# MLP's first product: the tail's low-by-high products as 64-row pairs

## The chip, the cores and the metric

The kernel runs on one core of one Trainium2 chip. The core has five engines with instruction queues of their own: TensorE (PE, matrix products, with its weight loads listed as PEld), VectorE (DVE), ScalarE (ACT), GpSimd (POOL) and SyncE (SP, which issues the DMAs). Engines run their queues in order and wait for each other by semaphores. The metric is the device time of one execution in microseconds (us); the time before is 894.02 us, the median of 3 runs from 894.0 to 894.94.

## The reference

Two pairs of layers: linear attention, then an MLP with gelu, each behind a layernorm and with a residual. S = 2048 tokens, D = 448, F = 1792, 16 heads of 28.

```python
def _B_ref(x, w1, b1, w2, b2):
    h = jnp.einsum("bsd,df->bsf", x, w1) + b1
    h = _gelu(h)
    return jnp.einsum("bsf,fd->bsd", h, w2) + b2
x = A_x
x = x + _A_ref(_layernorm(x, axis=-1), A_wqkv, A_wo)
x = x + _B_ref(_layernorm(x, axis=-1), B_w1, B_b1, B_w2, B_b2)
x = x + _A_ref(_layernorm(x, axis=-1), A_wqkv, A_wo)
x = x + _B_ref(_layernorm(x, axis=-1), B_w1, B_b1, B_w2, B_b2)
```

`_A_ref` is the linear attention. All arrays are float32.

## The kernel before

**Precision.** Every float32 operand of a large product is split into a high part, rounded to the type that TensorE takes at full speed (float32r), and a low part, the rest. A product a·b becomes three: hi·hi, hi·lo, lo·hi.

**Tiling.** D = 448 is contracted as three chunks of 128 rows and a tail of 64. For the tail, the activations hold the 64 rows twice, one copy over the other, and the weights hold hi over lo in 128 rows (`w1x`). So one product of 128 rows gives x_hi·(w_hi + w_lo), and a second one x_lo·(w_hi + w_lo), of which x_lo·w_lo is more than the three terms need.

**Stages of a layer.** Phase 1 goes over 16 token tiles of 128 for k, v and q (`proj`, `stage_g` and others), while w1 and w2 are loaded and split in the background (`bg_pieces`: ScalarE rounds the high part, GpSimd subtracts for the low one). A short transition turns the attention's sums into a matrix. Then the MLP runs over NB = 4 blocks b of 512 tokens, and in each block over NF = 14 chunks i of 128 columns of F:

- `mlp1(l, b, i)`: 11 products of 512 columns into one bank of PSUM, tag `h` with two banks taken in turn (L699 to L701 for the three chunks of D, L702 and L703 for the tail); then gelu on ScalarE into `g` (L705), its high part `gh` by a cast on ScalarE (L708, tag A, two buffers), its low part `gl` on VectorE (L709, tag B, two buffers).
- `mlp2(l, b, i, acc)`: 12 products of 448 columns, three for each of the four token tiles (L717, L718 with `gh`, L719 with `gl`), summed over the 14 chunks in four banks.
- `behind(l, b, i, tr)`: the attention's output and the layernorm of the next block (or the one behind it), a few steps in each i by a table written out by hand: `PLAN_0` for b = 0, `PLAN_1` for b = 1, `PLAN` for b = 2. Its steps: `z` (`q_z`, GpSimd), `p` (`q_prep`: VectorE scales q and turns it in 32x32 squares), `sq` and `lq` (to memory and back), `q` (`q_part`: the cast of qh on ScalarE and the subtraction for ql on VectorE, L269 and L270), `o` (`oc_mm`: 11 products, L651 to L655, then `o_ln` on VectorE, L660 and the statistics), `n` (`m_prep`: normalizes and turns, L190, L251, L252), `sx`, `lx` and `x` (`m_part`: the splits XH on ScalarE and XL on VectorE, L269 and L270, from which mlp1 of the next block reads). Of the plans: block 0 has "o1 n0 q2 ld0" at i = 6, "o2 n1 sx0 q3" at 7, "x1 p0 z1" at 11 and "x2 x3 p1 sq0 z2" at 12; block 1 has "o2 n1 sx0 q3" at 4, "o3 n2 lx0 ld0" at 5, "x2 p2 z3 lq0" at 10 and "x3 p3 sq1" at 11.

The order in each engine's queue is the order of the calls (the schedule is manual). In step i it is mlp1 of chunk i+1 (or of chunk 0 of the next block), `background(1)` in the first block of the first layer, the steps of `behind`, then mlp2 of chunk i.

Of the kernel before, what the change touches and what calls it, by code (L numbers as in the profile page):

```python
# [10 lines left out]
F32R = mybir.dt.float32r  # L11
AF = mybir.ActivationFunctionType
OP = mybir.AluOpType
# [9 lines left out]
def linear_attn_mlp_kernel(  # L23
# [12 lines left out]
    pe, act, dve, pool, sp = nc.tensor, nc.scalar, nc.vector, nc.gpsimd, nc.sync  # L36
    x0 = x_in[0]
    y_out = out[0]
    S, D = x0.shape
    F = w1.shape[1]  # L40
    H, DH = 16, 28
    NT = S // 128
    NB = NT // 4
    NF = F // 128
# [17 lines left out]
    def bank(tag, bufs, name):  # L62
        return psum.tile([128, 512], F32, name=name, tag=tag, bufs=bufs)
# [3 lines left out]
    def t448(tag, bufs, name, dt=F32):  # L67
        bufs = NH if tag == "H" else bufs
        return work.tile([128, D], dt, name=name, tag=tag, bufs=bufs)

    def t512(tag, bufs, name, dt=F32):
        return work.tile([128, 512], dt, name=name, tag=tag, bufs=bufs)

    def f(ap):
        return ap.bitcast(F32)
# [4 lines left out]
    def load_x(l, t):  # L80
        xt[l, t] = t448("H", 8, f"x{l}_{t}")
        sp.dma_start(xt[l, t], x_d[l][t * 128:(t + 1) * 128, :])
# [5 lines left out]
    def stage_piece(src, c, eng, s):  # L88

        if c < 3:  # L90
            eng.dma_start(s, src[c * 128:(c + 1) * 128, :])
        else:
            eng.dma_start(s[0:64], src[TL:D, :])
            eng.dma_start(s[64:128], src[TL:D, :])
        return s
# [69 lines left out]
    b1s = consts.tile([128, NF], F32, name="b1s")  # L165
# [4 lines left out]
    w1x = wts.tile([128, F], F32R, name="w1x")  # L170
# [44 lines left out]
    blocks = {}  # L215
# [80 lines left out]
    def bg_pieces():  # L296
        n = 0

        def stage():
            nonlocal n  # L300
            n += 1
            if n <= LATE:
                return t512("xn", 2, "stg")[:, :D]
            return t448(f"W{5 + n % 2}", 1, "stg")

        for fc in range(4):
            sl = slice(fc * D, (fc + 1) * D)
            for c in range(4):
                s = stage_piece(w1[:, sl], c, sp, stage())

                def go(c=c, s=s, sl=sl):
                    if c < 3:
                        act.copy(w1h[:, c, sl], s)
                        pool.tensor_tensor(w1l[:, c, sl], s, f(w1h[:, c, sl]), op=OP.subtract)
                    else:
                        tmp = t512("e", 3, "bx", F32R)[:, :D]
                        act.copy(tmp, s)
                        act.copy(w1x[0:64, sl], s[0:64])
                        pool.tensor_tensor(w1x[64:128, sl], s[64:128], f(tmp[64:128]), op=OP.subtract)
                yield go  # L320
        for i in range(NF):
            s = stage()
            sp.dma_start(s, w2[i * 128:(i + 1) * 128, :])

            def go(i=i, s=s):
                act.copy(w2h[:, i], s)
                pool.tensor_tensor(w2l[:, i], s, f(w2h[:, i]), op=OP.subtract)
            yield go
# [4 lines left out]
    def background(n):  # L333
        while bg_wait:
            bg_wait.pop(0)()
        for _ in range(n):
            g = next(bg, None)
            if g is not None:
                bg_wait.append(g)
# [78 lines left out]
    def stage_q(l, t):  # L418
        if t is None:
            return  # L420
        qo.append((l, t, proj("q", ("a", l, t // 4), t % 4)))
# [173 lines left out]
    def load_pq(l, b, j):  # L595
        t = b * 4 + j
        pqt[l, t] = t448(f"W{j}", 1, f"pq{l}_{t}")
        sp.dma_start(pqt[l, t], pq_d[l][t * 128:(t + 1) * 128, :])

    def q_z(l, b, j, tr):  # L600
        pz = pzs[l, b, j] = t448(f"W{4 if b else 4 + j % 2}", 1, "pz")
        pool.tensor_tensor(pz, pqt[l, b * 4 + j], tr.zb, op=OP.mult)  # L602
# [87 lines left out]

    gs = {}

    def mlp1(l, b, i):
        hp = bank("h", 2, "hp")
        s = slice(i * 128, (i + 1) * 128)
        x = blocks["m", l, b]
        o = hp.rearrange("p (t n) -> p t n", t=4)
        for c in range(3):
            pe.matmul(o, w1h[:, c, s], x.moving(x.hi, c), start=(c == 0), stop=False)  # L699
            pe.matmul(o, w1l[:, c, s], x.moving(x.hi, c), start=False, stop=False)  # L700
            pe.matmul(o, w1h[:, c, s], x.moving(x.lo, c), start=False, stop=False)  # L701
        pe.matmul(o, w1x[:, s], x.moving(x.hi, 3), start=False, stop=False)  # L702
        pe.matmul(o, w1x[:, s], x.moving(x.lo, 3), start=False, stop=True)  # L703
        g = t512("e", 3, "g")
        act.activation(g, hp, AF.Gelu_apprx_tanh, bias=b1s[:, i:i + 1])  # L705
        gh = t512("A", 2, "gh", F32R)
        gl = t512("B", 2, "gl", F32R)
        act.copy(gh, g)  # L708
        dve.tensor_sub(gl, g, f(gh))  # L709
        gs[i] = (gh, gl)  # L710

    def mlp2(l, b, i, acc):
        gh, gl = gs.pop(i)
        first, last = i == 0, i == NF - 1
        for j in range(4):
            s = slice(j * 128, (j + 1) * 128)
            pe.matmul(acc[j], gh[:, s], w2h[:, i], start=first, stop=False)  # L717
            pe.matmul(acc[j], gh[:, s], w2l[:, i], start=False, stop=False)  # L718
            pe.matmul(acc[j], gl[:, s], w2h[:, i], start=False, stop=last)  # L719
            if last:  # L720
                t = b * 4 + j
                xs = xt.pop((l, t))
                dve.tensor_tensor(xs, acc[j], xs, op=OP.add)
                sp.dma_start(x_d[l + 1][t * 128:(t + 1) * 128, :], xs)
# [95 lines left out]
    for l in range(LAYERS):  # L820
        tr = SimpleNamespace(mp={})
        za, acc = phase1(l, tr)
        if l == 0:
            background(0)
        fill = list(range(DEFER, NT))

        def pre(j):
            for k in range(4):
                load_pq(l, 1, k)
            q_z(l, 1, 0, tr)  # L830

        tok_ = SimpleNamespace(
            Q=lambda j: stage_q(l, fill.pop(0)), Qp=lambda j: stage_qphi(), G=lambda j: stage_g(l, NT - 1, acc),
            ld=lambda j: (load_pq(l, 0, j), load_x(l, j)), z=lambda j: trans_z(tr, za), gt=lambda j: trans_gt(tr, acc),
            kv=lambda j: trans_kv(tr), mask=lambda j: trans_mask(tr), m=lambda j: trans_m(tr, j),
            ms=lambda j: trans_ms(tr, j), qz=lambda j: q_z(l, 0, j, tr), qs=lambda j: q_scale(l, 0, j, tr),
            tq=lambda j: q_transpose(l, 0, j), qq=lambda j: q_split(l, 0, j), o=lambda j: o_mm(l, 0, j, tr),
            la=lambda j: o_ln(l, 0, j), lb=lambda j: o_n(l, 0, j), T=lambda j: m_transpose(l, 0, j),
            x=lambda j: m_split(l, 0, j), pre=pre)
        for tok in ORDER.split():  # L840
            name, j = tok.rstrip("0123456789"), int("0" + tok.lstrip("abcdefghijklmnopqrstuvwxyzQTG"))
            getattr(tok_, name)(j)
        assert not fill and not qo

        mlp1(l, 0, 0)
        trans_chunks(tr)
        for b in range(NB):
            acc = [bank("acc", 4, f"y{j}")[:, :D] for j in range(4)]
            nxt = b + 1 < NB
            if not nxt and l + 1 < LAYERS:  # L850
                st_k = stage_square(wqkv[:, D:2 * D])
                st_q = stage_square(wqkv[:, :D])
                load_to(l + 1, PRE - 1)
            for i in range(NF):
                if i + 1 < NF:
                    mlp1(l, b, i + 1)
                elif nxt:
                    mlp1(l, b + 1, 0)
                if l == 0 and b == 0:
                    background(1)  # L860
                if nxt:
                    behind(l, b, i, tr)
                elif l + 1 < LAYERS:
                    if i == 2:
                        split_kq("k", st_k)
                    if i == 5:
                        split_kq("q", st_q)
                    if i in (3, 4, 6, 7, 8):
                        t = (3, 4, 6, 7, 8).index(i)
                        stage_a(l + 1, t)  # L870
                        stage_n(l + 1, t)
                        stage_t(l + 1, t)
                        if t % 2:
                            stage_sp(l + 1, t)
                    if 9 <= i < 13:
                        stage_x(l + 1, i - 9)
                mlp2(l, b, i, acc)
# [28 lines left out]
```

## Time and profile before

| | |
|---|---|
| median of 3 runs | 894.02 us (894.0 to 894.94) |
| profiled execution | 896.46 us |
| its span on the core | 894.7 us |
| granted TensorE clock | 0.996 of full speed |
| instructions in the profile | 11665 |
| HBM traffic | 100 GB/s over the span |

The profile shows one execution. Its parts are the busy time of each engine, the chain of work that ended last (followed back from the last instruction to what released each step), groups of equal instructions with the idle time of the engine ahead of them and what ended it, and the timeline of single instructions: start in us, duration in us, engine, line, operation, output<-inputs, shape, count, and in brackets the idle time of the engine ahead of it and what released it. Matmuls overlap in the array: the recorded length of one is longer than the distance from its start to the next one's.

### The profile page before, as it was taken

The numbers are of one execution on the slowest core, as the hardware profiler recorded it, in microseconds if no ns is written. First come the engines' busy times: TensorE is split into PE (matmuls) and PEld (weight loads), VectorE is DVE, ScalarE is ACT, GpSimd is POOL, SyncE is SP. The second block draws the span as 40 slices with busy tenths as digits, with TensorE's granted clock in tenths as the row PEclk, the third lists the DMA queues.
The fourth block names the chain that finished last, engine by engine and source line by source line (L and its number), as shares of the span: only waits on it lengthen the run. The fifth ranks groups of instructions, "written<-read, shape, count | busy, mean of one in ns | idle before, by whom it ended". The sixth has DMA issues, their size and how long they took to land.

```text
span 894.7 us, 11665 instructions
## 1 busy us (share of the span) xinstructions
PE 878.8 (98%) x4184; PEld 772.8 (86%) x4184; DVE 502.3 (56%) x970; ACT 339.5 (38%) x586; POOL 209.1 (23%) x243
## 2 busy tenths in 40 slices
PE   7999999999999999999999999999999999999998
PEld 6898988888788888888889998888878888888887
DVE  6897686655754544226469866864565473532112
ACT  4677744333222322333345564343132233223221
POOL 4576723322112012002023333320310210210000
PEclk8999999999999999999999999999999999999999
DMA  6386622623513412051135542053233223010001
GB/s 175 121 244 220 194 82 92 208 76 102 170 52 92 143 33 80 16 175 48 47 127 196 173 123 82 32 178 112 65 106 132 91 92 130 34 62 20 22 1 42
DMA packets 62762, 93.71 MB, mean 105 GB/s; under 512 B 8816, under 2 KB 57968, under 8 KB 62704
## 3 DMA queue, kind: packets, MB, share of 16 engines
q1 hardware_dynamic: 62704, 92.97, 32.9%
q8 instruction: 33, 0.54, 0.3%
q14 instruction: 25, 0.20, 0.1%
HBM read 55.65 MB, written 34.08 MB: 100 GB/s over the span
## 4 chain that ended last, share of the span: by engine, by line
PE 84%; DVE 7%; issue 2%; DMA 2%; ACT 2%; POOL 2%; SPq 1%; POOLq 0%; DVEq 0%; ACTq 0%
PE y L719 10%; PE y L717 10%; PE y L718 10%; PE hp L701 8%; PE hp L700 8%; PE hp L699 8%; PE hp L703 3%; PE hp L702 3%; PE G L436 2%; PE G L437 2%; PE G L435 2%; PE op L652 2%; PE op L651 2%; PE op L653 2%; PE psk L281 2%
## 5 line engine op out<-in xcount | busy, mean ns | idle before, releaser
L709 DVE TENSOR_TENSOR gl<-g,gh 128x512 fp32r<-128x512 f32 x112 | 78.5, 701 | 303.6 <-ACT gh L708 303.5
L705 ACT ACTIVATE g<-hp,b1s 128x512 f32<-128x512 f32 x112 | 77.1, 688 | 400.7 <-PE hp L703 400.6
L717 PE MATMUL y<-w2h,gh 128*128 128x448 f32 x448 | 163.8, 366 | 1.7 <-ACT g L705 1.7
L719 PE MATMUL y<-w2h,gl 128*128 128x448 f32 x448 | 163.8, 366 | 0.5 <-DVE gl L709 0.5
L718 PE MATMUL y<-w2l,gh 128*128 128x448 f32 x448 | 163.6, 365 | 0.0
L701 PE MATMUL hp<-XL,w1h 128*128 128x512 f32 x336 | 131.3, 391 | 0.3 <-DVE XL L270 0.3
L699 PE MATMUL hp<-XH,w1h 128*128 128x512 f32 x336 | 131.5, 391 | 0.1
L700 PE MATMUL hp<-XH,w1l 128*128 128x512 f32 x336 | 131.6, 392 | 0.0
L183 POOL TENSOR_TENSOR brs<-bve,mhalf 128x1 f32<-128x1 f32 x64 | 39.8, 622 | 320.4 <-DVE bve L181 318.3
L717 PEld LDWEIGHTS y<-w2h,gh 128*128 128x128 f32 x448 | 84.1, 188 | 11.4 <-ACT g L705 2.5
L718 PEld LDWEIGHTS y<-w2l,gh 128*128 128x128 f32 x448 | 84.1, 188 | 8.3
L719 PEld LDWEIGHTS y<-w2h,gl 128*128 128x128 f32 x448 | 84.2, 188 | 7.5 <-DVE gl L709 0.9
L701 PEld LDWEIGHTS hp<-XL,w1h 128*128 128x128 f32 x336 | 63.1, 188 | 14.8 <-DVE XL L270 1.2
L699 PEld LDWEIGHTS hp<-XH,w1h 128*128 128x128 f32 x336 | 63.1, 188 | 11.8 <-ACT XH L269 0.8
L700 PEld LDWEIGHTS hp<-XH,w1l 128*128 128x128 f32 x336 | 63.1, 188 | 11.2
L708 ACT CAST gh<-g 128x512 fp32r<-128x512 f32 x112 | 69.7, 622 | 3.6
L602 POOL TENSOR_TENSOR pz<-pq,zb 128x448 f32<-128x448 f32 x32 | 37.1, 1162 | 105.2 <-DVE dn L608 74.0
L666 POOL TENSOR_TENSOR x<-x,b2b 128x448 f32<-128x448 f32 x32 | 36.9, 1152 | 31.5 <-DVE xm L190 23.3
L702 PE MATMUL hp<-XH,w1x 128*128 128x512 f32 x112 | 43.6, 389 | 0.0
L703 PE MATMUL hp<-XL,w1x 128*128 128x512 f32 x112 | 43.6, 389 | 0.0
L177 DVE BATCH_NORM_STATS2 bst<-x 128x6 f32<-128x448 f32 x64 | 39.8, 622 | 6.3 <-DMA x<-in_A_x_dram 5.2
L389 POOL TENSOR_TENSOR xnl<-x,xnh 128x384 fp32r<-128x384 f32 x32 | 35.4, 1107 | 29.6 <-ACT xnh L388 23.0
(144 smaller groups left out, 1581.1 us busy)
## 6 DMA issues: line engine op xcount, KB each, us to landing
x<-in_A_x_dram SPq DMA_DIRECT2D x32, 224.0 KB, 4.0
pq_d<-eq SPq DMA_DIRECT2D x32, 224.0 KB, 2.2
pq<-pq_d SPq DMA_DIRECT2D x32, 224.0 KB, 3.2
x<-x_d SPq DMA_DIRECT2D x32, 224.0 KB, 3.3
sq_a<-sq SPq DMA_DIRECT2D x13, 512.0 KB, 2.6
sp<-sq_a SPq DMA_DIRECT2D x52, 128.0 KB, 3.0
sq_q<-sq SPq DMA_DIRECT2D x12, 512.0 KB, 2.6
sp<-sq_q SPq DMA_DIRECT2D x48, 128.0 KB, 3.0
```

Source lines behind the costliest of these rows:

```text
L177: dve.bn_stats(st, xs)
L699: pe.matmul(o, w1h[:, c, s], x.moving(x.hi, c), start=(c == 0), stop=False)
L700: pe.matmul(o, w1l[:, c, s], x.moving(x.hi, c), start=False, stop=False)
L701: pe.matmul(o, w1h[:, c, s], x.moving(x.lo, c), start=False, stop=False)
L702: pe.matmul(o, w1x[:, s], x.moving(x.hi, 3), start=False, stop=False)
L703: pe.matmul(o, w1x[:, s], x.moving(x.lo, 3), start=False, stop=True)
L705: act.activation(g, hp, AF.Gelu_apprx_tanh, bias=b1s[:, i:i + 1])
L708: act.copy(gh, g)
L709: dve.tensor_sub(gl, g, f(gh))
L717: pe.matmul(acc[j], gh[:, s], w2h[:, i], start=first, stop=False)
L718: pe.matmul(acc[j], gh[:, s], w2l[:, i], start=False, stop=False)
L719: pe.matmul(acc[j], gl[:, s], w2h[:, i], start=False, stop=last)
```

## The change

The two products of the tail stay, but the second (x_lo) takes only the 64 rows of `w1x` that hold the high part. It is put off until two chunks have their other 10 products, and then both chunks' 64-row products are issued one behind the other. So that the two lie in different halves of the array's rows, `w1x` holds hi over lo in chunks of even number and lo over hi in chunks of odd number. The x_lo·w_lo term of those chunks is no longer computed. The two gelus are issued after the pair.

`mlp1_ahead` replaces the call of mlp1 in step i. It brings forward one chunk more: steps 0, 2, 4, 6, 8 and 10 end with the pair (i+1, i+2), ahead of `behind` and of mlp2(i). For blocks 1 and 2 chunk 13 pairs with chunk 0 of the next block at i = 12, and chunk 1 of the next block is begun at i = 13. Chunk 0 of blocks 0 and 1 and chunk 13 of blocks 0 and 3 keep the whole product (`whole`). That is 26 pairs and 4 whole products in each layer.

In the background work the tail of w1 comes in pieces of 512, 512, 512 and 256 columns instead of four of 448, and each is split in two turns (even chunks, odd chunks).

```diff
-                        tmp = t512("e", 3, "bx", F32R)[:, :D]
+                        tmp = t512("e", 3, "bx", F32R)[:, :sl.stop - sl.start]
                         act.copy(tmp, s)
-                        act.copy(w1x[0:64, sl], s[0:64])
-                        pool.tensor_tensor(w1x[64:128, sl], s[64:128], f(tmp[64:128]), op=OP.subtract)
+                        o, a, h = (v.rearrange("p (k u n) -> p k u n", u=2, n=128) for v in (w1x[:, sl], s, tmp))
+                        for u in range(2):
+                            hi, lo = slice(u * 64, u * 64 + 64), slice(64 - u * 64, 128 - u * 64)
+                            act.copy(o[hi, :, u], a[hi, :, u])
+                            pool.tensor_tensor(o[lo, :, u], a[lo, :, u], f(h[lo, :, u]), op=OP.subtract)
...
-    def mlp1(l, b, i):
-        hp = bank("h", 2, "hp")
+    hps = {}
+
+    def mlp1(l, b, i, whole=False):
+
+        hp = hps[b, i] = bank("h", 2, "hp")
...
         pe.matmul(o, w1x[:, s], x.moving(x.hi, 3), start=False, stop=False)
-        pe.matmul(o, w1x[:, s], x.moving(x.lo, 3), start=False, stop=True)
+        if whole:
+            pe.matmul(o, w1x[:, s], x.moving(x.lo, 3), start=False, stop=True)
+            gelu(b, i)
+
+    def mlp1_pair(l, *ends):
+
+        for b, i in ends:
+            x, rows = blocks["m", l, b], slice(i % 2 * 64, i % 2 * 64 + 64)
+            pe.matmul(hps[b, i].rearrange("p (t n) -> p t n", t=4), w1x[rows, i * 128:(i + 1) * 128],
+                      x.moving(x.lo, 3)[rows], start=False, stop=True)
+        for b, i in ends:
+            gelu(b, i)
+
+    def gelu(b, i):
         g = t512("e", 3, "g")
-        act.activation(g, hp, AF.Gelu_apprx_tanh, bias=b1s[:, i:i + 1])
+        act.activation(g, hps.pop((b, i)), AF.Gelu_apprx_tanh, bias=b1s[:, i:i + 1])
         gh = t512("A", 2, "gh", F32R)
         gl = t512("B", 2, "gl", F32R)
         act.copy(gh, g)
         dve.tensor_sub(gl, g, f(gh))
         gs[i] = (gh, gl)
 
+    def mlp1_ahead(l, b, i):
+
+
+        joined = 1 <= b < NB - 1
+        if i == 0:
+            if not 1 < b:
+                mlp1(l, b, 1)
+            mlp1(l, b, 2)
+            mlp1_pair(l, (b, 1), (b, 2))
+        elif i < 11 and i % 2:
+            mlp1(l, b, i + 2)
+        elif i < 11:
+            mlp1(l, b, i + 2)
+            mlp1_pair(l, (b, i + 1), (b, i + 2))
+        elif i == 11:
+            mlp1(l, b, 13, not joined)
+        elif i == 12 and joined:
+            mlp1(l, b + 1, 0)
+            mlp1_pair(l, (b, 13), (b + 1, 0))
+        elif i == 13 and joined:
+            mlp1(l, b + 1, 1)
+        elif i == 13 and b + 1 < NB:
+            mlp1(l, b + 1, 0, True)
...
-        mlp1(l, 0, 0)
+        mlp1(l, 0, 0, True)
...
             for i in range(NF):
-                if i + 1 < NF:
-                    mlp1(l, b, i + 1)
-                elif nxt:
-                    mlp1(l, b + 1, 0)
+                mlp1_ahead(l, b, i)
```

More of the change, by code (lines that the diff above doesn't have):

```diff
@@ L297, in bg_pieces, with stage @@
         n = 0
-        def stage():
+        def stage(wd=D):
             nonlocal n
@@ L302, in stage @@
             if n <= LATE:
-                return t512("xn", 2, "stg")[:, :D]
+                return t512("xn", 2, "stg")[:, :wd]
             return t448(f"W{5 + n % 2}", 1, "stg")
         for fc in range(4):
-            sl = slice(fc * D, (fc + 1) * D)
             for c in range(4):
-                s = stage_piece(w1[:, sl], c, sp, stage())
+                wd = D if c < 3 else 512
+                sl = slice(fc * wd, min((fc + 1) * wd, F))
+                s = stage_piece(w1[:, sl], c, sp, stage(wd)[:, :sl.stop - sl.start])
                 def go(c=c, s=s, sl=sl):
```

## The prediction

> **What bounds the kernel now.** I read the head of the page first, then the chain of waits, the groups of instructions, and the timeline of each engine around the places that the change touches.
>
> ```profile
> span 894.7 us, 11665 instructions
> PE 878.8 (98%) x4184; PEld 772.8 (86%) x4184; DVE 502.3 (56%) x970; ACT 339.5 (38%) x586; POOL 209.1 (23%) x243
> PE 84%; DVE 7%; issue 2%; DMA 2%; ACT 2%; POOL 2%; SPq 1%; POOLq 0%; DVEq 0%; ACTq 0%
> L709 DVE TENSOR_TENSOR gl<-g,gh 128x512 fp32r<-128x512 f32 x112 | 78.5, 701 | 303.6 <-ACT gh L708 303.5
> L708 ACT CAST gh<-g 128x512 fp32r<-128x512 f32 x112 | 69.7, 622 | 3.6
> L703 PE MATMUL hp<-XL,w1x 128*128 128x512 f32 x112 | 43.6, 389 | 0.0
> ```
>
> TensorE sets the end: 98% busy and 84% of the chain. VectorE (56%) looks free, but it holds 7% of the chain, so there are places where TensorE waits for it. What one product costs is the distance between starts, not its recorded length:
>
> ```profile
> 311.27 0.36 PE L717 MATMUL y<-w2h,gh 128*128 128x448 f32 x1
> 313.70 0.39 PE L699 MATMUL hp<-XH,w1h 128*128 128x512 f32 x1
> 316.21 0.36 PE L717 MATMUL y<-w2h,gh 128*128 128x448 f32 x1
> ```
>
> From 311.27 to 313.70 stand the 12 products of mlp2: 0.2025 us each, 2.43 together. From 313.70 to 316.21 stand the 11 of mlp1: 0.228 each. So an L703 product costs 0.228, though its record is 0.389 long.
>
> **The change part by part.** *The half products.* The change takes no instruction from TensorE: 26 pairs a layer, 52 in all, replace two L703 products of 128 rows by two of 64 rows, in the two halves of the array and two banks. The other 8 of the 112 stay whole. If both halves run fully together, a pair costs 0.228 instead of 0.456: 52 × 0.228 = 11.9 us saved. If they run one after the other, nothing is saved. No row of this trace shows a 64-row product, so the value lies between, and the nearest rows are those where the array's weights change fast or late:
>
> ```profile
> 140.49 0.36 PE L283 MATMUL psq<-wq,XL 128*128 128x448 f32 x1
> 140.69 0.60 PE L228 MATMUL tp<-ident,xm 128*128 128x128 f32 x4
> L228 PE MATMUL tp<-ident,xm 128*128 128x128 f32 x32 | 4.9, 276 | 1.0 <-DVE xm L190 0.6 <-DVE XL L235 0.4
> 89.48 0.47 PE L436 MATMUL G<-kl,xnh 128*128 128x448 f32 x1
> 89.79 0.36 PE L437 MATMUL G<-kh,xnl 128*128 128x448 f32 x1
> ```
>
> Four transposes of 128 columns span 0.60 and one lasts 0.276, so they start (0.60 - 0.276) / 3 = 0.108 apart. At 89.48 a product that had waited lasts 0.47 instead of 0.36, and the next starts 0.31 later instead of 0.20. Both say the same: a weight load that nothing hides costs about 0.11. I take it that the second half's weights load only once the first half has started: the pair costs 0.11 + 0.228 and saves 0.118, 52 × 0.118 = 6.1 us. For the other end I take a full drain where the array goes from whole to half and back: each exposes 0.389 - 0.228 = 0.161, so a pair that is otherwise perfect loses 0.322 - 0.228 = 0.094, 4.9 us in all.
>
> The Trainium skill, TensorEngine Tiling (Array Packing), Key Properties, says that a change of tiling mode, as against a change of tile, drains the TensorE. No run here shows such a change yet; by that rule the pairs would lose the 4.9 us. The Trainium skill, TensorE: Matmul & The Clock Gate, Part 3 (The mechanism), has matmuls in different row groups start about 4 ns apart; by that one they would save the 11.9.
>
> *The new wait.* Pairs form two chunks at a time, so both gelus of a pair are issued after it. The tiles gh and gl have two buffers each, which chunks take in turn. At even i the pair (i+1, i+2) stands ahead of mlp2(i), so the cast of gh for chunk i+2 takes the buffer that mlp2(i) still reads; in the changed program's order that cast waits for the L718 product of the fourth output in mlp2(i), the 11th of 12. Before, gh for i+1 took the buffer of i-1, whose readers were done. Behind the waiting cast stand, on ScalarE, all casts of the work for the next block; behind gl on VectorE stand o_ln, the turn of m_prep and the split ql of q_part. TensorE waits for ql and for XL. With T as the start of mlp2(i): the 11th product starts at T + 10 × 0.2025, ends 0.36 later, the cast takes 0.62, and with two handovers of 0.03 gl starts at T + 3.07.
>
> *Place a: o2 in block 0 (i=7), o3 in block 1 (i=5).* Before, in the same step:
>
> ```profile
> 186.62 0.69 DVE L709 TENSOR_TENSOR gl<-g,gh 128x512 fp32r<-128x512 f32 x1 [0.76 <-ACT gh L708]
> 187.47 0.62 DVE L660 TENSOR_TENSOR x<-op,x 128x448 f32<-128x448 f32 x1 [0.16 <-PE op L655]
> ...
> 190.12 0.27 DVE L252 STREAM_TRANSPOSE sq<-xm 128x128 f32<-128x128 f32 x1
> 190.31 1.35 DVE L270 TENSOR_TENSOR ql<-sp,qh 128x512 fp32r<-128x512 f32 x1
> 187.27 0.37 PE L717 MATMUL y<-w2h,gh 128*128 128x448 f32 x1
> 192.63 0.36 PE L653 MATMUL op<-wq,ql 128*128 128x448 f32 x1
> ```
>
> From the start of gl to the end of ql: 191.66 - 186.62 = 5.04, less the 0.16 in which VectorE waited for TensorE, 4.88. TensorE needs ql at 192.63: only 0.97 to spare, although the engine is 56% busy. In the change gl starts at T + 3.07 and ql ends at T + 7.95, while TensorE wants it after mlp2 (2.43), ten products of mlp1 (2.28) and two of oc_mm (0.41), at T + 5.12. It waits 2.83, and 0.11 more for the weights: 2.94. The other ten ql of a layer are issued in an odd step, a step earlier, or with no o_ln ahead of them, and fit. Twice a layer: 5.9.
>
> *Place b: the first chunk of block 1.* Before:
>
> ```profile
> 218.03 0.69 DVE L709 TENSOR_TENSOR gl<-g,gh 128x512 fp32r<-128x512 f32 x1 [3.65 <-ACT gh L708]
> 218.65 0.69 DVE L270 TENSOR_TENSOR XL<-sp,XH 128x512 fp32r<-128x512 f32 x1
> ...
> 222.10 0.27 DVE L252 STREAM_TRANSPOSE sq<-pq 128x128 f32<-128x128 f32 x1
> 222.98 0.69 DVE L709 TENSOR_TENSOR gl<-g,gh 128x512 fp32r<-128x512 f32 x1 [0.60 <-ACT gh L708]
> 223.58 1.29 DVE L270 TENSOR_TENSOR XL<-sp,XH 128x512 fp32r<-128x512 f32 x2
> 223.63 0.37 PE L719 MATMUL y<-w2h,gl 128*128 128x448 f32 x1
> 224.04 0.51 PE L699 MATMUL hp<-XH,w1h 128*128 128x512 f32 x1
> 224.38 0.39 PE L700 MATMUL hp<-XH,w1l 128*128 128x512 f32 x1
> 224.93 0.50 PE L701 MATMUL hp<-XL,w1h 128*128 128x512 f32 x1 [0.15 <-DVE XL L270]
> 225.27 0.40 PE L699 MATMUL hp<-XH,w1h 128*128 128x512 f32 x1
> 231.85 0.39 PE L703 MATMUL hp<-XL,w1x 128*128 128x512 f32 x1
> 233.09 0.44 PE L717 MATMUL y<-w2h,gh 128*128 128x448 f32 x1 [0.86 <-ACT g L705]
> 233.37 0.36 PE L718 MATMUL y<-w2l,gh 128*128 128x448 f32 x1
> ```
>
> Already now this start loses 0.21 + 0.11 + 0.32 + 0.11 (starts from 223.63 to 225.27, less 0.2025 or 0.228 each) = 0.75, and the first gelu of the block another 1.02 + 0.08 = 1.10. The second goes away, because two chunks of mlp1 now stand ahead of mlp2(0). The first grows: gelu(13) is issued at i=11, so gh and gl of chunk 13 wait for mlp2(11), and behind gl stand the split x1, the whole q_prep and the splits x2 and x3. From 218.03 to 222.37 that chain takes 4.34, the last two splits 1.32: x3 is done at T + 3.07 + 5.66 = T + 8.73. TensorE wants it after mlp2(11), mlp2(12) and two products, T + 5.32. It waits 3.41 + 0.11 = 3.5. Net of the two old waits: 3.5 - 0.75 - 1.10 = 1.65.
>
> *Place c: from block 1 to block 2.* There the first chunk of the next block is taken at i=12, one step earlier than before. With T the start of mlp2(10), x3 is done at T + 3.07 + 4.34 + 0.03 + 0.68 = T + 8.12; wanted at 2.43 + 2.28 + 2.43 + 0.46 = T + 7.60. It waits 0.5 + 0.1 = 0.6. Block 3's first chunk has no q_prep ahead of it, and loses nothing.
>
> Together 5.9 + 1.65 + 0.6 = 8.15 a layer, 16.3 in both.
>
> *The split of w1's tail* in phase 1:
>
> ```profile
> L319 POOL TENSOR_TENSOR w1x<-stg,bx 64x448 fp32r<-64x448 f32 x4 | 4.6, 1156 | 0.3
> L390 POOL TENSOR_TENSOR xnh<-x,xnh 128x64 fp32r<-128x64 f32 x32 | 14.9, 466 | 0.0
> ```
>
> Four subtractions become eight, six of 256 columns and two of 128. Between 0.466 at 64 and 1.156 at 448 columns, 256 give 0.81 and 128 give 0.58: 6.0 us instead of 4.6, and four more casts on ScalarE. It lies beside phase 1's products; if TensorE comes to wait for POOL it costs up to the 1.4 plus the casts, at most 2, at least 0. I take 0.6.
>
> Sum: +16.3 + 0.6 - 6.1 = +10.8 us. The profiled execution has a span of 894.7 and took 896.46 in all; the median of the runs is 894.02, so the sum goes on that: 894.0 + 10.8 = 904.8, say 905.
>
> **The rivals.** *Halves fully side by side:* 894.0 + 16.9 - 11.9 = 899. For it: the two halves use different rows and banks, and weight loads run under products everywhere in this trace. Against it: no load here is ever two ahead of its product. *The change doesn't do what it says, the halves follow one another:* 894.0 + 16.9 = 911. For it: the two products stand one behind the other in one queue, as all do here; against it: nothing that they use is shared. *Drains at both borders:* 894.0 + 16.9 + 4.9 = 916. For it: every record here is 0.161 longer than its slot, so something is still in the array when the next product enters. Against it: the transposes at 140.69, another use of the array, start right behind the last product (140.49 + 0.20). (The Trainium skill's rule on tiling modes, named above, is this case.) *Faster:* VectorE and ScalarE take the late gl without TensorE noticing, as their shares (56% and 38%) and the 303.6 us in which VectorE idles ahead of gl suggest. Then places a and c cost nothing, the start of block 1 keeps its 0.75 and loses its 1.10 twice: 894.0 + 0.6 - 6.1 - 2.2 = 886. It decides for faster wherever the added waits stay under what the pairs save, that is if gl's delay of some 3.7 us past its old place (start at T - 0.65, now T + 3.07) finds that much slack in the chains behind it. The 0.97 us at ql speaks against it.
>
> **How the numbers follow.** Partly hidden second half, 905: 0.35, with 902 to 908 as its own range. Fully side by side, 899: 0.25. One after the other, 911: 0.15. Drains, 916: 0.17. No added waits, 886: 0.08. The range from 898 to 917 leaves out the last and some tails. A measurement of this kernel tells 0.2% (1.8 us) from no change; slower has the first four, 0.92 less 0.02 for the side-by-side case with waits that come out 4 us smaller: slower 0.90, same 0.02, faster 0.08.
>
> **What would show it.** Pairs: the distance from the first half's start to the next whole product, 0.34 by the forecast, 0.23 to 0.24 side by side, 0.46 in sequence, 0.55 with drains. Waits: at even i the cast of gh for chunk i+2 idles until mlp2(i) ends; four waits of about 3 us for ql at the third product of oc_mm, two of about 3.5 us for XL at the start of block 1, and the 1.1 us wait for the first gelu of block 1 gone. TensorE's busy share falls, and VectorE and ScalarE do about the same work. I would be wrong if ql is ready in time in block 0, or if pairs cost more than two whole products.

## The result, and the profile after

| | before | after |
|---|---|---|
| median | 894.01 us (893.9 to 894.94, 4 runs) | 925.86 us (924.71 to 931.32, 4 runs) |
| ratio | | 1.0367, 95% interval 1.0346 to 1.0387 |
| profiled execution, its span | 896.46, 894.7 us | 925.37, 923.7 us |
| granted TensorE clock over the span | 0.996 | 0.989 |

The change makes the kernel 3.7% slower. The forecast was 905 us, with a range from 898 to 917: the sign was right, the time lies outside. The medians differ by 31.9 us, the spans of the two profiled executions by 28.9; what follows is read from these two.

The head of the page, the chain of waits and four groups of the changed kernel (line, engine, operation, out<-in, shape, count, then busy us and mean ns of one, then the engine's idle us ahead of it and what ended it):

```profile
span 923.7 us, 11660 instructions
PE 892.0 (97%) x4184; PEld 763.9 (83%) x4184; DVE 503.3 (54%) x970; ACT 334.8 (36%) x590; POOL 207.9 (23%) x247
PE 79%; DVE 12%; issue 3%; ACT 2%; DMA 2%; SPq 2%; POOL 1%; DVEq 0%; POOLq 0%; ACTq 0%
L729 ACT CAST gh<-g 128x512 fp32r<-128x512 f32 x112 | 69.5, 620 | 63.6 <-issue 33.3
L709 PE MATMUL hp<-XL,w1h 128*128 128x512 f32 x336 | 132.6, 395 | 7.0 <-DVE XL L270 7.0
L658 PE MATMUL op<-wq,ql 128*128 128x448 f32 x72 | 27.1, 376 | 10.8 <-DVE ql L270 10.6 <-DMA stg<-in_B_w_dram 0.2
L719 PE MATMUL hp<-XL,w1x 64*128 64x512 f32 x104 | 25.7, 491 | 0.0
```

Three things stand in these lines. The cast of gh has 63.6 us of idle time ahead of it where it had 3.6: it stands at the head of ScalarE's queue and waits for its buffer (the timeline below shows one). TensorE waits 10.6 us for ql and 7.0 us for XL, and VectorE's share of the chain has gone from 7% to 12%, though VectorE does no more work (503.3 us against 502.3). And a half product's record is 0.491 us long against 0.389 for a whole one. L719 has 104 products in 25.7 busy us: as busy time counts overlap once, they run together, and yet TensorE's busy time has risen from 878.8 to 892.0.

A pair in the timeline of TensorE and of its weight loads (start us, length, engine, line; "x2" merges the two halves):

```profile
336.14 0.39 PE L710 MATMUL hp<-XH,w1x 128*128 128x512 f32 x1
336.46 0.49 PE L719 MATMUL hp<-XL,w1x 64*128 64x512 f32 x2
336.88 0.47 PE L656 MATMUL op<-wq,qh 128*128 128x448 f32 x1
337.19 0.36 PE L657 MATMUL op<-wq,qh 128*128 128x448 f32 x1
```

```profile
335.92 0.19 PEld L710 LDWEIGHTS hp<-XH,w1x 128*128 128x128 f32 x1
336.46 0.18 PEld L719 LDWEIGHTS hp<-XL,w1x 64*128 64x128 f32 x2 [0.35 <-issue]
336.88 0.19 PEld L656 LDWEIGHTS op<-wq,qh 128*128 128x128 f32 x1 [0.24 <-issue]
```

Before, each product's weights load while the product ahead of it runs. Here the load of L719 starts with its own product at 336.46, and that of L656 with its own at 336.88: twice the loader sits idle and the load is exposed. By the single records the two halves start 0.003 to 0.004 us apart in all 52 pairs. From L710 to L719 pass 0.318 us instead of 0.228, from L719 to the next whole product 0.424, and from that to the next 0.309 instead of 0.203. That is 1.051 us where the four slots of before took 0.2275 × 3 + 0.2025 = 0.885: a pair costs 0.166 more than two whole products, 52 × 0.166 = 8.6 us.

The late gl, in block 0 at o2: the last product that reads gh's buffer on TensorE (L763, the 11th of mlp2(6)), the waiting cast on ScalarE, VectorE's timeline, and TensorE's wait for ql:

```profile
192.38 0.36 PE L763 MATMUL y<-w2l,gh 128*128 128x448 f32 x1
192.83 0.62 ACT L729 CAST gh<-g 128x512 fp32r<-128x512 f32 x1 [2.77 <-issue]
```

```profile
193.48 0.69 DVE L730 TENSOR_TENSOR gl<-g,gh 128x512 fp32r<-128x512 f32 x1 [3.29 <-ACT gh L729]
194.09 0.62 DVE L665 TENSOR_TENSOR x<-op,x 128x448 f32<-128x448 f32 x1
...
196.73 0.27 DVE L252 STREAM_TRANSPOSE sq<-xm 128x128 f32<-128x128 f32 x1
196.92 1.32 DVE L270 TENSOR_TENSOR ql<-sp,qh 128x512 fp32r<-128x512 f32 x1
```

```profile
198.30 0.48 PE L658 MATMUL op<-wq,ql 128*128 128x448 f32 x1 [2.66 <-DVE ql L270]
```

The cast starts 0.09 us after that product's recorded end. VectorE sits idle for 3.29 us, starts gl at 193.48 and ends ql at 198.24, 4.76 us later; TensorE has been waiting since 195.6.

After the longest waits comes something that the forecast did not have. The start of block 1, and two windows of time (from:to, length, busy us and count of PE, PEld, DVE, ACT and POOL, granted clock PEclk with 1.00 as full, DMA share, GB/s):

```profile
231.46 0.79 PE L709 MATMUL hp<-XL,w1h 128*128 128x512 f32 x1 [3.18 <-DVE XL L270]
232.05 0.63 PE L707 MATMUL hp<-XH,w1h 128*128 128x512 f32 x1
232.47 0.63 PE L708 MATMUL hp<-XH,w1l 128*128 128x512 f32 x1
232.90 0.63 PE L709 MATMUL hp<-XL,w1h 128*128 128x512 f32 x1
...
234.46 0.40 PE L710 MATMUL hp<-XH,w1x 128*128 128x512 f32 x1
234.69 0.40 PE L712 MATMUL hp<-XL,w1x 128*128 128x512 f32 x1
```

```profile
231.00:235.00 4.00, 3.54 (x10) 2.83 (x11) 3.30 (x7) 0.00 (x0) 1.14 (x1) 0.59 0.00 0
241.00:245.00 4.00, 4.00 (x20) 3.15 (x19) 2.03 (x4) 1.90 (x4) 0.00 (x0) 1.00 0.63 230
```

Behind the wait the products start 0.427 apart instead of 0.228, and the granted clock is 0.59 in these 4 us. This happens behind four of the waits, with 1.3 to 1.6 us lost each time (the distances over their usual ones, added up), 6.0 us in all.

Which waits are followed by it can be read from the same trace. Its low stretches behind waits begin at 230.86, 278.65, 650.70 and 684.83 us, whole multiples of 3.41 us apart, and each lasts 3.41 us at 0.50. Windows on that grid, with TensorE's busy time alone (from:to, length, busy us and count, PEclk, DMA share, GB/s):

```profile
196.73:200.14 3.41, 1.84 (x9) 1.00 0.00 0
227.45:230.86 3.41, 0.82 (x4) 1.00 0.00 0
230.86:234.28 3.42, 2.83 (x7) 0.50 0.00 0
275.24:278.65 3.41, 1.40 (x7) 1.00 0.37 154
278.65:282.06 3.41, 3.41 (x11) 0.50 0.61 167
725.79:729.21 3.42, 1.70 (x8) 1.00 0.00 0
```

A window with 2.01 us of idle time (275.24) is followed by one at half clock, a window with 1.72 us (725.79) is not. In the three traces that have these waits (this one, and e1 and e5 below) all 12 full-clock windows between 50 and 880 us with 2.01 us or more of idle time are followed by a half-clock one, and none with 1.72 us or less. So a wait of 2.82 us costs clock only where most of it falls into one window, in 6 of 12 cases; the waits of 3.35 us did in 6 of 6.

### The profile page after: what moved, and what is told of

Read it like the earlier page. It is cut to its first block, busy times and chain, and to the rows that moved or that the text cites. A ratio compares the mean times of both kernels' runs of the same rounds, so it can differ in the third digit from the quotient of the medians.

```text
span 923.7 us, 11660 instructions
## 1 busy us (share of the span) xinstructions
PE 892.0 (97%) x4184; PEld 763.9 (83%) x4184; DVE 503.3 (54%) x970; ACT 334.8 (36%) x590; POOL 207.9 (23%) x247
## 4 chain that ended last, share of the span: by engine, by line
PE 79%; DVE 12%; issue 3%; ACT 2%; DMA 2%; SPq 2%; POOL 1%; DVEq 0%; POOLq 0%; ACTq 0%
PE y L762 9%; PE y L763 9%; PE y L764 9%; PE hp L709 7%; PE hp L708 7%; PE hp L707 7%; PE hp L710 2%; PE hp L719 2%; PE G L442 2%; PE G L441 2%; PE G L440 2%; PE op L658 2%; PE op L656 2%; PE psk L280 2%; PE psk L281 2%
## 5 line engine op out<-in xcount | busy, mean ns | idle before, releaser
L762 PE MATMUL y<-w2h,gh 128*128 128x448 f32 x448 | 169.2, 378 | 0.0
L763 PE MATMUL y<-w2l,gh 128*128 128x448 f32 x448 | 164.6, 367 | 0.0
L729 ACT CAST gh<-g 128x512 fp32r<-128x512 f32 x112 | 69.5, 620 | 63.6 <-issue 33.3
L763 PEld LDWEIGHTS y<-w2l,gh 128*128 128x128 f32 x448 | 85.1, 190 | 7.2
L709 PEld LDWEIGHTS hp<-XL,w1h 128*128 128x128 f32 x336 | 63.6, 189 | 22.3 <-DVE XL L270 8.8
L707 PEld LDWEIGHTS hp<-XH,w1h 128*128 128x128 f32 x336 | 63.5, 189 | 10.8
L710 PE MATMUL hp<-XH,w1x 128*128 128x512 f32 x112 | 43.8, 391 | 0.0
L279 PE MATMUL psk<-wk,XH 128*128 128x448 f32 x96 | 35.9, 374 | 3.2 <-ACT XH L234 3.2
```

## The experiments

All times are medians; the kernel before ran beside them at 895.95 us (13 runs) for e1 to e4 and 894.77 us (one run) for e5 and e6, against 894.01 beside the changed kernel, so a difference between these sets is good to some 2 us. A visit means that the array goes from whole products to half ones and back.

**e1: whole products in the pairs.**

```diff
-            pe.matmul(hps[b, i].rearrange(...), w1x[rows, i * 128:(i + 1) * 128],
-                      x.moving(x.lo, 3)[rows], start=False, stop=True)
+            pe.matmul(hps[b, i].rearrange(...), w1x[:, i * 128:(i + 1) * 128],
+                      x.moving(x.lo, 3), start=False, stop=True)
```

> The changed order with both products of a pair over all 128 rows again (x_lo times hi and lo, as before the change). Theory 'borders': 52 pairs cost 0.166 us each more than two whole products (0.318 + 0.424 + 0.309 in the place of 0.228 + 0.455 + 0.203), so 8.6 us go: 925.9 - 8.6 = 917 us, and the late gl waits stay as they are (two of 2.8 us at ql, one of 3.35 us at XL in each layer). Rival 'the order does it all': the pairs cost nothing, 925 us.

Measured: 917.28 us, ratio to before 1.024 (1.0217 to 1.0262). The waits stand as they did: four for ql (2.82 us each by the distances) and two for XL (3.35). So the half products as such cost some 8.6 us, and the order of the calls the rest. That the medians meet the 8.6 so closely is partly luck: e1's four runs go from 915.53 to 919.51, and its profiled execution has five half-clock windows behind waits where the changed kernel's has four. (e3 and e4 below give the same price without such windows.) In this run one wait of 2.82 us is followed by a low clock and the other in the same layer, which a window's border cuts in two, is not (windows of the first kind above, from 199.0 and from 279.2 us):

```profile
199.00:203.00 4.00, 3.94 (x12) 3.51 (x13) 0.56 (x2) 0.00 (x0) 0.00 (x0) 0.57 0.00 0
279.20:283.00 3.80, 3.80 (x19) 3.54 (x20) 1.57 (x5) 0.00 (x0) 0.00 (x0) 1.00 0.51 174
```

**e2: half products without pairs**, in the kernel before.

```diff
-        pe.matmul(o, w1x[:, s], x.moving(x.lo, 3), start=False, stop=True)
+        pe.matmul(o, w1x[0:64, s], x.moving(x.lo, 3)[0:64], start=False, stop=True)
```

> The kernel before with its last tail product of each chunk over the 64 rows of w1's high part alone (the term x_lo times w_lo is left out), no pair, order unchanged: 112 visits to half the array, one product each. Theory 'borders': a visit costs as much with one half as with two, because the second is free: one product in each visit starts 0.32 us after the product ahead of it, 0.42 us pass to the next whole product, and that lasts 0.10 us longer; + 0.39 us x 112 = 44 us, 938 us. Rival 'two halves slow each other': a single half costs a plain slot of 0.23 us, 894 us.

Measured: 939.96 us, one run (span 938.2, 43.5 over before's). TensorE's timeline around one of them:

```profile
158.50 0.39 PE L702 MATMUL hp<-XH,w1x 128*128 128x512 f32 x1
158.81 0.50 PE L703 MATMUL hp<-XL,w1x 64*128 64x512 f32 x1
159.24 0.47 PE L717 MATMUL y<-w2h,gh 128*128 128x448 f32 x1
159.55 0.37 PE L718 MATMUL y<-w2l,gh 128*128 128x448 f32 x1
```

Alone, a half product takes what a pair takes: 0.31, 0.43 and 0.31 us. A visit costs the same with one product as with two, so the second is free and the visit is what costs.

**e3: the second gelu behind mlp2.**

```diff
-        for b, i in ends:
-            gelu(b, i)
+        gelu(*ends[0])
+        late.append(ends[1])
...
                 mlp2(l, b, i, acc)
+                while late:
+                    gelu(*late.pop())
```

Chunk 13 of blocks 0 and 3 goes the same way.

> The changed kernel with the gelu, gh and gl of a pair's second chunk (and of chunk 13 where it stands alone) issued behind mlp2(i) in place of ahead of the next block's work, so that no cast waits for a buffer at the head of the queue. Theory 'late gl': all waits of 2.8 and 3.35 us go, and the drops of the clock behind them too; the pairs' 8.6 us stay; the 1.1 us wait for the first gelu of block 1 stays away: 894 + 8.6 - 2.2 to - 3.7 = 899 to 900 us. Rival 'VectorE is simply too full in these steps': the waits stay, 920 us or more.

Measured: 899.18 us, ratio 1.0037 (1.0022 to 1.0051), 0.4% longer than before. The pairs are all there, with the same distances, and from the first to the last product of the MLP TensorE has no gap but theirs. The list of TensorE's waits has eleven entries left, all of phase 1 and the transition; its first lines (engine, line, what it waited for, us in total, times, longest), and the group of the casts of gh:

```profile
PE psk L279 <- ACT XH L234: 2.7, 1, 2.7
PE warm L149 <- POOL ident masks.py:199: 1.4, 1, 1.4
```

```profile
L729 ACT CAST gh<-g 128x512 fp32r<-128x512 f32 x112 | 69.5, 621 | 47.9 <-issue 27.7
```

The cast still waits for its buffer (47.9 us of idle time, 63.6 in the changed kernel), but the next block's work now stands ahead of it in the queue, and TensorE no longer notices. The mean clock is 0.996 again. VectorE was not too full; it was held up from another engine's queue. e3 moves gelu, cast and gl together: that it is the cast that waits is read from the timeline at 192.83, not from a run that moves it alone.

**e4: e1 and e3 together.**

> Both: whole products in the pairs, the second gelu behind mlp2(i). Both theories together: nothing is left but the order of two chunks ahead, which spares the 1.1 us wait for the first gelu of block 1 and perhaps the 0.75 us for XL, in each layer: 890.5 to 892 us, faster than before. If a wait of another kind stays in the order: over 894 us.

Measured: 890.82 us (890.62 to 892.47, 6 runs), ratio 0.9948 (0.9932 to 0.9964): 0.5% shorter than before, with the interval clear of 1. e3 and e4 differ in the pairs alone, both at mean clocks of 0.995 to 0.998: 899.18 - 890.82 = 8.4 us is the price of the 52 pairs, without any low clock. Both MLP stages by windows:

```profile
147.60:450.80 303.20, 303.20 (x1420) 266.41 (x1419) 154.06 (x292) 94.64 (x157) 51.46 (x51) 1.00 0.32 97
581.70:885.00 303.30, 303.30 (x1421) 266.43 (x1419) 133.24 (x252) 85.81 (x139) 36.27 (x36) 1.00 0.24 76
```

TensorE is busy in all of 303.2 and 303.3 us, at full clock; before, these stages took 306.0 and 305.3 from their first product to their last. What is left of the change here is two chunks of mlp1 ahead instead of one, which spares the waits at the start of block 1 and one of 0.69 us for gl in the first layer. That is some 4.7 of the 5.8 us by which the span is shorter than before; most of the rest lies between the MLP stages, and its cause is open (see below the last table).

**e5: both halves of a pair in rows 0 to 63.**

```diff
-                            hi, lo = slice(u * 64, u * 64 + 64), slice(64 - u * 64, 128 - u * 64)
+                            hi, lo = slice(0, 64), slice(64, 128)
...
-            x, rows = blocks["m", l, b], slice(i % 2 * 64, i % 2 * 64 + 64)
+            x, rows = blocks["m", l, b], slice(0, 64)
```

> The changed kernel with w1's tail as hi over lo in all chunks, so that both products of a pair use rows 0 to 63 of the array. Theory 'borders, halves side by side': the second half no longer starts 0.003 us after the first but a plain slot of 0.23 us, at most 0.33 where its weights show, later; nothing else in the visit changes; + 12 to 17 us on the changed kernel, 938 to 943 us. Rival 'the array takes one 64-row product at a time in any place': the same as the changed kernel, 925 us, second start at 0.003.

Measured: 939.65 us, one run.

```profile
165.67 0.39 PE L710 MATMUL hp<-XH,w1x 128*128 128x512 f32 x1
165.98 0.73 PE L719 MATMUL hp<-XL,w1x 64*128 64x512 f32 x2
166.64 0.47 PE L762 MATMUL y<-w2h,gh 128*128 128x448 f32 x1
```

The two now span 0.73 us instead of 0.49. By the single records the second starts 0.335 us after the first in each pair, and not 0.003: it is the two halves of the array that let them run together. 0.335 is a slot of 0.228 and 0.107 of weights, the upper of the two values expected. That fits a load that is not hidden either, because it goes into the rows that are in use.

**e6: two pairs in one visit**, in block 3 of each layer, on e3.

```diff
+            if i in (2, 6):
+                mlp1(l, b, i + 2)
+                mlp1(l, b, i + 3, tag="m")
+                mlp1(l, b, i + 4, tag="m")
+                mlp1_pair(l, *((b, i + k) for k in (1, 2, 3, 4)))
```

> Late gelu (e3), and in block 3 of each layer chunks 3 to 6 and 7 to 10 give their four 64-row products in one visit (two more banks). Theory 'borders': a visit costs 0.39 us once, whatever it holds, and each further pair 0.23: the third product starts 0.23 us after the first, the next whole one 0.65 us after it; against two whole products per pair the visit then saves 0.455 x 2 - 0.455 - 0.167 - 0.228 = 0.06 us. Rival 'a 64-row product is slow in itself': the third starts 0.42 us after the first, the next whole one 0.85 us after it. On the whole time (4 visits) about 1 us either way, which the time cannot tell.

Measured: 902.02 us, one run; that is 2.8 us over e3, of which 3.3 lie outside the MLP stages (149.7 us to the first one and 132.4 between them, against 148.1 and 130.7) and -0.4 in them, so the whole time tells nothing, as expected. In the second layer's stage, where no new wait comes in, it is 0.75 us under e3 (306.60 against 307.35); in the first layer's TensorE waits once for gl, 0.64 us at 415.51. The visit:

```profile
408.51 0.39 PE L710 MATMUL hp<-XH,w1x 128*128 128x512 f32 x1
408.83 0.73 PE L719 MATMUL hp<-XL,w1x 64*128 64x512 f32 x4
409.50 0.47 PE L776 MATMUL y<-w2h,gh 128*128 128x448 f32 x1
409.81 0.37 PE L777 MATMUL y<-w2l,gh 128*128 128x448 f32 x1
```

Neither number that I had expected came out: the third half starts 0.338 us after the first (0.23 by "borders", 0.42 by the rival), and the next whole product 0.664 after it. That is e5's distance again: the border is paid once, and each further pair costs a slot and an exposed weight load. Four half products in one visit take 0.318 + 0.664 + 0.309 = 1.29 us from L710 on, where whole ones take 0.228 × 5 + 0.203 = 1.34. From two pairs in a visit on, half products gain, by 0.05 us. Two such visits in place of four with one pair each come to 2 × (0.33 + 0.05) = 0.76 us a layer, which is what the second layer's stage shows.

## Why the prediction failed

The sum by its terms, against the spans of the two profiled executions (waits and clock from the distances between starts):

| term | forecast | measured |
|---|---|---|
| 52 pairs against 104 whole products | -6.1 | +8.6 |
| waits in the MLP, net of the old ones | +16.3 | +15.8 |
| lower clock behind the waits | not in the sum | +6.0 |
| phase 1, and the stretch between the MLPs | +0.6 | +0.3 and -1.4 |
| together | +10.8 | +29.3; the spans differ by 28.9 |

The -1.4 is not a wait: in the 86 us behind the first layer's MLP the products of 448 columns follow 0.2027 us apart in the changed kernel and 0.2067 before. It does not go with the order of the calls alone: e5, in the changed order, has 0.2039 there, and e6, in that order but for block 3, has 0.2067. Its cause is open.

**The step that failed is the price of a pair**: "the pair costs 0.11 + 0.228 and saves 0.118". Its premise, that the second half's weights load only once the first half has started, holds for two products in the same rows (e5: 0.335) and not for two in different halves of the array, which start 0.003 apart. On that point the rival "fully side by side" had it right. But the visit costs 0.395 us around it, in four parts. The sum is measured between starts; the split uses the recorded lengths, whose ends are modelled, and is an estimate: 0.091 before the first half may start, 0.102 for its weights (0.491 against 0.389), 0.095 before the next whole product may start (0.424 less 0.228 and 0.102), 0.107 for that one's weights. Two halves together save one slot of 0.228, and 0.395 - 0.228 = 0.167 is lost. e2 shows the same visit with one product in it. The sign that the prediction named, the distance from the first half to the next whole product, is 0.424 and looks like "0.46 in sequence"; it can't tell the cases apart, because one border's cost lies ahead of the first half. With the pair's price alone put right the sum would have been 919.5 us, with the clock alone 910.8.

**The bound was too narrow for the same reason.** The worst case for a pair, a loss of 0.094 us, came from two drains of 0.161. By the split above the drains are smaller, 0.09 each, but each border also exposes a weight load. I had both prices from rows (0.161 and 0.11) and used one in the forecast and the other in the rival, as if only one of them could hold; the records show both at each border, as the loads of L719 and L656 start only with their own products. The two together would have given 0.322 + 0.22 - 0.228 = 0.31, a bound on the safe side. The Trainium skill, TensorEngine Tiling (Array Packing), Key Properties, had the drain: the trace agrees that the change of shape costs time, by the split some 0.09 us a border. The Trainium skill, TensorE: Matmul & The Clock Gate, Part 3 (The mechanism), had the start 4 ns apart: the trace agrees, at 3 to 4 ns. Both held at once.

**The waits were right in mechanism, place and size.** With 0.10 to 0.11 for the weights behind each: place a 2.82 + 0.10 = 2.93 (2.94 forecast), four times; place b 3.35 + 0.11 = 3.46 (3.5), twice; place c 0.50 + 0.11 = 0.61 (0.6), twice; the 1.1 us for the first gelu of block 1 is gone. Not foreseen were a wait of 0.33 + 0.10 at o1 of the first layer's block 0, and that an old one there of 0.69 + 0.10 for gl went away; these two partly cancel, which is luck. e3 shows the cause by taking it away: with the second gelu behind mlp2 no wait of these is left.

**The clock was missing.** The forecast added waits of 2.9 and 3.5 us and left the clock at 1.00. Behind both waits at place b and behind two of the four at place a, TensorE ran 3.41 us at half the clock. In e3 and e4, without the waits, the mean clock is 0.996 and 0.998. The windows of three traces part cleanly by their idle time (2.01 us and more, 1.72 and less), but no run sets that time by itself, and where between the two the border lies is open. Where the windows fall differs between the traces (counted back to the start in steps of 3.41 us, a border lies at 2.17 us in the changed kernel's and at 1.57 in e1's), so the 6.0 us belong to the profiled execution: of the four runs of the changed kernel three had mean clocks of 0.989 to 0.990 and took 924.71 to 926.35 us, the fourth had 0.983 and took 931.32.

**The rivals.** "Drains at both borders", 916, was the nearest: right in kind, short by the weights and the clock. "One after the other" falls with the 0.003 us, "faster" with the waits for ql.

## What to carry to other kernels

Half-array products run side by side, but the change of shape is what is paid: count visits and not products, and here it takes two pairs in a visit to come out ahead. When work is brought forward, look at which buffer it takes and who still reads it: one cast put ahead of its buffer's last reader held up two engines' queues, whose busy shares of 36% and 54% said nothing of it, and putting it, with its gelu and gl, behind that reader was worth 26.7 us here (925.86 - 899.18, low clock included). Where two prices for the same border stand in the trace, ask whether both hold at once before using them as two cases.

## What the hardware showed that I had not expected

- In the small shape no weight load is hidden under a product in the same rows: products follow 0.335 us apart (e5) and 0.338 (e6) where whole ones follow 0.228 apart, while a load for the other half of the array costs 0.003.
- A gap of 2.82 us on TensorE was followed by half-rate products in two of four cases in the changed kernel, a gap of 3.35 us in both; what decided was how much of the gap fell into one of the fixed windows. The Trainium skill, TensorE: Matmul & The Clock Gate, Part 1 (What's actually happening), has the clock halve after an idle window of about 3.4 us; the trace agrees on the half rate (0.427 us between starts against 0.228) and on a window of 3.41 us, but here 2.01 us of idle time within one were enough.
